# Two of four early loads asked for sooner, and batch 0's opening in a new order

## The chip, the cores and the metric

The kernel runs on one core of a Trainium2 chip. A core has five engines that run side by side, each working through its own list of instructions in order: TensorE (PE in the profile, with the loading of its weights shown as PEld), VectorE (DVE), ScalarE (ACT), GpSimd (POOL) and SyncE (SP). They meet through semaphores. Transfers between the core's memory and the chip's main memory run on 16 DMA engines; in this kernel POOL asks for the loads and SP for the copies inside the core and for the stores. The metric is the device time of one execution in microseconds (us), lower being better.

## The reference

The input x has 4 batches of 12480 rows of 128 numbers; there are 32 inducing rows I of 128 numbers and two weight matrices, w_in (128 x 2048) and w_out (2048 x 128).

```
h   = softmax(scale * I @ x^T) @ x          # per batch: 32 rows of 128
y   = softmax(scale * x @ h^T) @ h          # per batch: 12480 rows of 128
u   = y @ w_in                              # 49920 rows of 2048
out = (u * clip(u + 3, 0, 6) / 6) @ w_out   # 49920 rows of 128
```

Every row of y is a mixture of the 32 rows of h, with softmax weights. For small u the clip does nothing and the last two lines are a linear and a quadratic form of y. The kernel uses this: per batch it makes a table from h and the weights once (a linear part BD and a quadratic part Cq), and then needs for each row only products of the row's mixing weights with that table. A second path, taken only if a check of bounds at the end fails, computes everything directly; it isn't run on these inputs.

## The kernel before, in words

**Tiling.** A batch is cut into seven groups: six of 2048 rows (one load of 1 MB each) and one of 192 rows. A group of 2048 rows is four chunks of 512 rows, so that a batch has 25 chunks and the whole kernel 100.

**Three kinds of work.** *First pass* over a batch: load a group (load_x, line 207), cast it to bf16 (a_cast, line 357, written "k"), transpose it on TensorE into a bank of PSUM (a_T, line 366, "T") and copy it out (a_xT, line 375, "xT"), scores (a_scores, line 381, "s"), exponential (a_exp, line 393, "a"), and the weighted sum of rows (a_agg, line 419, "g"). After the last group this gives the denominators ("den", "n", line 403 and 451), H and its transpose HT (lines 467 to 482, with a bf16 copy HTb that ScalarE makes).
*Table* of a batch: 16 blocks, each a product dpm with a quarter of a column block of w_in (c_dpm, line 616, "dp"), its square ("q", line 631 on ScalarE, or lines 628 and 629 as a copy and a product on VectorE for the blocks named in BY_DVE), and four products with w_out (c_C, line 642, "C") into one bank cp; beside them G (line 517), hs (570, 571), L (585, 596), lt (601) and BD (606). The weights are first cast: w_in to bf16 ("wi", line 250, ScalarE), the rest that the cast leaves ("wl", line 255), w_out to bf16 ("wo", line 259).
*Second pass*: for each chunk the mixing weights TF (products bp, line 783, exponential at line 796), their products TD with d (line 807), and nine groups of products into a bank op (lines 818 and 837), which line 857 multiplies by r and line 867 stores. d is the bf16 tile dk of a group (line 762) spread over partitions by a copy inside the core that SP asks for (b_spread, line 771), six chunks ahead.

**Order.** Nothing is scheduled by a tool: each engine runs what the program text names, in that order. Batch 0's first pass and table, and the first pass of batch 1's group 0, come from the list ORDER, one token per step ("k5.1:A" is the cast of quarter 1 of group 5 on ScalarE, :D VectorE, :P GpSimd). After ORDER comes the loop over the 100 chunks ("the main loop"); it takes the second pass of chunk t and, from the list PLAN, pieces of the first pass and the table of the next batch at fixed places. In the loop SP asks at step t for the copy d of chunk t + 6.

**Banks.** TensorE writes into PSUM banks of three pools: five banks "f" (psF), two banks "o" (psO) and one for the weighted sum. In ORDER the last letter of a token on TensorE says from which pool its bank comes. A pool hands out its banks again only when the reader of the older content is done.

**Idle products.** "warmN:f" puts N products of 128x512 on a tile of zeros (line 278) into the list of TensorE, into a bank of the pool that is named; nobody reads them.

**Loads.** Five buffers of 1 MB hold loaded groups. POOL asks for batch 0's groups 1 to 4 at the start, and for groups 5 and 6 ("dx5", "dx6"), for batch 1's group 0 ("dx10"), w_in ("dwi", two halves) and w_out ("dwo", four quarters) as buffers come free. Batch 1's groups 1 to 4 are "held": the token "held" makes POOL copy one element of d of chunk 3 (the tile "seen", line 873), which waits until that copy has landed, and only then asks for the four loads. The next loads in PLAN are batch 1's group 6 in step 0 of the main loop and group 5 in step 1.

Of the kernel before, what the change touches and what calls it, by code (L numbers as in the profile page):

```python
# [28 lines left out]
LEAD = 2  # L29
AHEAD = 6  # L30
SUMG = 5
BY_DVE = (2, 6, 11)

SPLIT = (4, 5)

# [57 lines left out]
""".split()  # L93

ORDER = """
k0.0:A k0.2:D k0.1:A warm3:o T0.1:o T0.0:o xT0.1:A xT0.0:D k1.2 warm3:f s0:f a0 k1.0:D k1.1:P
T1.1:f z1:D z0:A T1.0:f z3:P xT1.1:D z2:A g0.0 xT1.0:D k2.1:P k2.2 g0.1 k2.0:D s1:f dx5 y0
T2.1:f a1 dx6 T2.0:o xT2.1:D g1.0 g1.1 k3.0:D k3.2 k3.1:D y1 dx10 T3.0:o xT2.0:A dwi warm2:f
s2:f T3.1:f dwo k4.0:D k4.1:A xT3.0:D a2 T4.0:f xT3.1:D k4.3:A g2.0 k4.2:A xT4.0:D s3:f T4.1:f
y2 a3 g2.1 xT4.1:A y3 g3.0 g3.1 s4:o k5.0:D k5.1:A k5.3:D k6:A warm2:o T5.0:o k5.2:D a4 T6:f  # L100
T5.1:f xT5.0:D xT6:A g4.0 xT5.1:D s5.0:f g4.1 y4 a5.0 bk2:P s5.1:f bk0:A s6:f g5.0 bk3:P dred
a5.1 a6 n5.0 bk1:P n5.1 wi0 g5.1 g6 n6 den bT0:o wl0:P rD H wl1:P bx0:A dall warm1:f htp:f bT1:o
HT Wd HTb bx1:D wi1 warm1:f pe1:ff HTl dH bs:f dk1 wl4:P pe0:fo W ba wo1:P dp13:o e1 dp6:f by
bg0 made wl7:P e0 q6 bg1 dk0 wo3:P dp5:f q13 sp0:f wl2:P spread0 dp15:f q5 dp2:f nf0 C6 wl3:P
C13 q15 q2 dp4:o wo0:P G0:o q4 C5 dp1:f dp0:f C15 q1 wl5:D held bp0.0:f wl6:D dp11:o q0 G1 q11
G2 TF0.0 C4 wo2:A G3 dp8:f C1 hs dp9:f q8 C0 dp14:f q9 bp0.1:f C11 C8 TF0.1 dp12:o cmax dp3:f C9
q12 half L0:f q14 L1 q3 dp10:f C2 L dp7:o TD0 q10 lt:o C3 q7 C12 BD C10 C14 C7 bp1.1:f rp0:f Cq
rp1 bp1.0:f TF1.1 TF1.0 warm2:f r0
""".split()


# [17 lines left out]
def kernel(  # L129
# [9 lines left out]
    P = nc.NUM_PARTITIONS  # L139
# [30 lines left out]
    with ExitStack() as es:  # L170
# [29 lines left out]
        def load_x(b, g):  # L200
            t0, p, n = groups[g]
            src = x[b, t0 : t0 + p * n, :].rearrange("(p i) c -> p i c", i=n)
            if n == TG:
                t = xin.tile([P, TG, C], FP32R, name="xr")
            else:
                t = xlast.tile([P, n, C], FP32R, name="xl")
            nc.gpsimd.dma_start(t[:p, :, :], src)
            xs[(b, g)] = t
# [13 lines left out]
        held = [1, 2, 3, 4]  # L222
# [86 lines left out]
        BD = []  # L309
# [49 lines left out]
        def a_T(b, g, h, how="f"):  # L359
            t0, p, n = groups[g]  # L360
            st = S[b]
            lo, hi = (0, n // 2) if h == 0 else (n // 2, n)
            xb = xbs[(b, g)]
            pt = bank(how, [P, 1024], BF16, "pt")
            for i in range(lo, hi):
                nc.tensor.transpose(pt[:, (i - lo) * p : (i - lo + 1) * p], xb[:p, i, :], ident_b[:p, :p])  # L366
            st[("pt", g, h)] = pt

        def a_xT(b, g, h, eng):
            t0, p, n = groups[g]  # L370
            lo, hi = (0, n // 2) if h == 0 else (n // 2, n)
            if ("xT", g) not in S[b]:
                S[b][("xT", g)] = (xTp if n == TG else xTl).tile([P, n * p], BF16, name="xT")
            pt = S[b].pop(("pt", g, h))
            eng(S[b][("xT", g)][:, lo * p : hi * p], pt[:, : (hi - lo) * p])  # L375

        def a_scores(b, g, how="f", lo=0, hi=TG):
            t0, p, n = groups[g]
            s1 = bank(how, [P, 512], FP32, "s1")
            for i in range(lo, min(hi, n)):  # L380
                nc.tensor.matmul(  # L381
                    s1[:p, i * M : (i + 1) * M],
                    lhsT=S[b][("xT", g)][:, i * p : (i + 1) * p],
                    rhs=I_T[:, :],
                )
            S[b][("s1", g, lo)] = s1
# [235 lines left out]
        def c_sq(jb):  # L622
            st = S[0]
            dpm = st.pop(("dpm", jb))
            sq = sqp.tile([P, 512], BF16, name="sq")
            if jb in BY_DVE:
                d32 = cst.tile([P, 512], FP32, name="d32", tag="scr")
# [251 lines left out]
        def first(kind, ix, how):  # L879
# [4 lines left out]
            i, j = (ix + [0, 0])[:2]  # L884
# [19 lines left out]
            elif kind == "T":  # L904
                a_T(0, i, j, at)
            elif kind == "xT":
                a_xT(0, i, j, eng)
            elif kind == "s":
                a_scores(0, i, at, *((8 * j, 8 * j + 8) if i == 5 else ()))
            elif kind == "a":  # L910
                a_exp(0, i, *((8 * j, 8 * j + 8) if i == 5 else ()))
            elif kind == "g":
                for h in range(2) if i == last else (j,):
                    a_agg(0, i, h)
            elif kind == "y":
                a_sum(0, i)
            elif kind == "n":
                a_den(i, *((8 * j, 8 * j + 8) if i == 5 else ()))
            elif kind == "dx":
                load_x(*((1, 0) if i == 10 else (0, i)))  # L920
            elif kind == "dwi":
                load_w_in()
            elif kind == "dwo":
                load_w_out(0, 4)
            elif kind == "held":
                gate("seen", S[0][("d", 3)][:, 0:1])
                while held:
                    load_x(1, held.pop(0))
            elif kind == "made":
                gate("made", S[0]["dH"][:, 1, 1, 0, 0:1])  # L930
            elif kind == "wi":
                w_in_cast(i)
            elif kind == "wo":
                w_out_cast(i, eng)
            elif kind == "wl":
                w_low(i, nc.vector if how == "D" else nc.gpsimd)
            elif kind == "bk":
                a_cast(1, 0, ((eng, i, i + 1),))
            elif kind == "bT":
                a_T(1, 0, i, at)  # L940
            elif kind == "bx":
                a_xT(1, 0, i, eng)
            elif kind == "bs":
                a_scores(1, 0, at)
            elif kind == "ba":
                a_exp(1, 0)
            elif kind == "bg":
                a_agg(1, 0, i)
            elif kind == "by":
                a_begin(1)  # L950
                a_sum(1, 0)
            elif kind == "dred":
                c_sum(0)
            elif kind == "HTb":
                c_HTb(0, act)
            elif kind == "htp":
                c_htp(0, at)
            elif kind in ("den", "rD", "dall", "H", "HT", "HTl", "W", "Wd"):
                {"den": c_den, "rD": c_rD, "dall": c_d, "H": c_H, "HT": c_HT, "HTl": c_HTl, "W": c_W, "Wd": c_Wd}[
                    kind  # L960
                ](0)
            elif kind == "dH":
                c_dH()
            elif kind == "pe":
                b_ep(0, i, at[0])
                b_pp(0, i, at[1])
            elif kind == "e":
                b_e(0, i)
            elif kind == "dk":
                b_dk(0, i)  # L970
                if i and "spread" in S[0]:
                    spread_rest()
            elif kind == "spread":
                for c in range(4):
                    b_spread(0, c)
                S[0]["spread"] = True
                if ("dk", 1) in S[0]:
                    spread_rest()
            elif kind == "sp":
                b_sp(0, i, at)  # L980
            elif kind == "nf":
                b_nf(0, i)
            elif kind == "rp":
                b_rp(0, i, at)
            elif kind == "r":
                b_r(0, 1)
            elif kind == "bp":
                b_bp(0, i, j, at)
            elif kind == "TF":
                b_TF(0, i, j)  # L990
            elif kind == "TD":
                b_prod(0, i)
            elif kind == "dp":
                c_dpm(i, at)
            elif kind == "q":
                c_sq(i)
            elif kind == "C":
                c_C(0, i)
            elif kind == "G":
# [331 lines left out]
```

## Time and profile before

| | us |
|---|---|
| median of 3 runs | 293.96 (293.09 to 295.51) |
| the profiled execution | 292.84 |
| its span, first to last instruction | 291.1 |
| TensorE busy in the span | 282.1 (97%) |
| VectorE busy | 231.9 (80%) |
| ScalarE busy | 227.0 (78%) |
| GpSimd busy | 130.5 (45%) |
| time around the span | 1.7 |

The page of the profile gives busy time per engine, then the chain that ended last, then the costliest groups. Two further views are used: a table of windows, which shows for each stretch of time the busy time of every engine and what the DMA engines moved, and the list of instructions in order of time, which shows when each started, how long it took, and after what idle time and whose release. Times in them count from the start of the span. A matmul's recorded duration contains its way through the array, so that several overlap; the distance from one start to the next is what it costs TensorE. The main loop starts at 42.2 us with the product of line 667 behind the last two idle products.

### The profile page before, as it was taken

How to read it: one execution, taken by the hardware profiler on the slowest of the kernel's cores; microseconds unless marked ns; L12 is line 12 of the kernel's file. 1: busy time of each engine (PE TensorE's matmuls, PEld its weight loads, DVE VectorE, ACT ScalarE, POOL GpSimd, SP SyncE). 2: the span in 40 equal slices, each digit the busy share in tenths (PEclk: the TensorE clock that was granted, in tenths of full speed). 3: DMA queues.
4: the chain of work that ended last, by engine and by line, in shares of the span. 5: the costliest groups of instructions: out<-in, count | busy, mean ns of one | idle time of the engine just before them, and what ended most of it. 6: DMA issues, size and time to landing. Idle time of an engine off the chain costs nothing.

```text
span 291.1 us, 9807 instructions
## 1 busy us (share of the span) xinstructions
PE 282.1 (97%) x3960; PEld 227.6 (78%) x3971; DVE 231.9 (80%) x495; ACT 227.0 (78%) x412; POOL 130.5 (45%) x250
## 2 busy tenths in 40 slices
PE   7999999899999999999999999999999999999993
PEld 2778667798888887978888786987887877787882
DVE  1777987789878887788898877788888887898784
ACT  2897988886889988888889887667789878777770
POOL 7465645111538899521677776100577850000000
PEclk9999999999999999999999999999999999999998
DMA  7999499698895665999838825616456566466764
GB/s 258 428 365 270 104 329 402 231 273 281 285 357 161 245 199 177 336 317 259 295 84 216 305 100 148 214 35 203 160 150 182 172 208 222 146 216 217 229 227 156
DMA packets 25137, 66.69 MB, mean 229 GB/s; under 512 B 3168, under 2 KB 18304, under 8 KB 19072
## 3 DMA queue, kind: packets, MB, share of 16 engines
q1 hardware_dynamic: 18880, 39.40, 41.9%
q0 software_dynamic: 6160, 26.61, 28.5%
q8 instruction: 32, 0.52, 0.7%
q14 instruction: 17, 0.14, 0.2%
q10 hardware_dynamic: 48, 0.02, 0.0%
HBM read 27.67 MB, written 25.56 MB: 183 GB/s over the span
## 4 chain that ended last, share of the span: by engine, by line
PE 80%; DMA 11%; DVE 5%; issue 1%; ACT 1%; ACTq 0%; DVEq 0%; POOLq 0%
PE op L837 29%; PE bp L783 13%; PE op L818 8%; PE hnd L419 7%; PE pt L366 5%; DMA xr<-in_x_dram 5%; PE cp L642 5%; DMA out_dram<-os 4%; PE s L381 2%; DMA d<-dk 2%; PE sp L687 2%; PE pp L748 2%; PE ep L667 2%; PE lp L585 1%; PE gp L517 1%
## 5 line engine op out<-in xcount | busy, mean ns | idle before, releaser
L796 ACT ACTIVATE TF<-bp 128x512 bf16<-128x512 f32 (+1 forms) x200 | 115.6, 589 | 32.8 <-PE bp L783 18.9
L837 PE MATMUL op<-Cq,TF 128*128 128x128 bf16 (+1 forms) x784 | 100.3, 221 | 0.1
L837 PE MATMUL op<-Cq,TD 128*128 128x128 bf16 (+1 forms) x784 | 98.6, 219 | 0.0
L857 DVE TENSOR_TENSOR os<-op,r_all 128x512 f32<-128x512 f32 x96 | 65.9, 687 | 20.5 <-PE op L837 18.3
L807 DVE TENSOR_TENSOR TD<-TF,d 128x1024 bf16<-128x1024 bf16 (+1 forms) x100 | 74.8, 748 | 0.2
L837 PEld LDWEIGHTS <-TF 128*128 128x128 bf16 (+1 forms) x784 | 56.1, 98 | 21.2 <-issue 11.0
L783 PE MATMUL bp<-xT,W 128*128 128x512 bf16 (+1 forms) x193 | 72.3, 375 | 0.1
L837 PEld LDWEIGHTS <-TD 128*128 128x128 bf16 (+1 forms) x784 | 60.4, 98 | 0.0
L818 PE MATMUL op<-BD,nf 128*128 128x512 f32 (+1 forms) x100 | 54.7, 547 | 0.0
L357 POOL CAST xb<-xr 128x512 bf16<-128x512 f32 x33 | 25.1, 778 | 29.7 <-DMA xr<-in_x_dram 17.5
L544 POOL COPY gate<-TD 128x1 bf16<-128x1 bf16 x48 | 14.1, 294 | 51.2 <-DVE TD L807 49.2
L547 POOL TENSOR_TENSOR dg<-G 128x256 f32<-128x256 f32 x48 | 35.6, 741 | 0.0
L546 POOL TENSOR_TENSOR dg<-G 128x256 f32<-128x256 f32 x48 | 31.5, 656 | 6.9 <-DVE r_all L736 3.6
L554 ACT ACTIVATE sq<-dg 128x512 bf16<-128x512 f32 x48 | 30.0, 629 | 3.8 <-POOL dg L547 2.1
L419 PE MATMUL hnd<-xr,a 128*32 128x128 f32 x384 | 30.6, 227 | 0.0
L366 PE MATMUL pt<-ident_b,xb 128*128 128x128 bf16 x392 | 29.6, 219 | 1.0 <-DVE xb L357 0.5
L419 PEld LDWEIGHTS hnd<-xr,a 128*32 128x32 f32 x384 | 24.8, 109 | 2.7 <-issue 1.3
L366 PEld LDWEIGHTS <-xb 128*128 128x128 bf16 x392 | 23.2, 98 | 4.6 <-issue 1.6
L726 PE MATMUL rp<-one,nf 128*128 128x4 f32 (+1 forms) x100 | 25.6, 257 | 0.9 <-ACT dk L762 0.9
L375 ACT COPY xT<-pt 128x1024 bf16<-128x1024 bf16 (+1 forms) x24 | 22.4, 950 | 2.8 <-PE pt L366 2.6
L642 PE MATMUL cp<-w_out_b,sq 128*128 128x128 bf16 x256 | 22.4, 220 | 0.1
L726 PEld LDWEIGHTS rp<-one,nf 128*128 128x128 f32 (+1 forms) x100 | 18.9, 189 | 3.7 <-ACT dk L762 1.3
(131 smaller groups left out, 417.2 us busy)
## 6 DMA issues: line engine op xcount, KB each, us to landing
xr<-in_x_dram POOLq DMA_DIRECT2D x23, 1024.0 KB, 8.1
out_dram<-os SPq DMA_DIRECT2D x23, 1024.0 KB, 4.6
d<-dk SPq DMA_DIRECT2D x96, 128.0 KB, 4.4
os<-in_x_dram SPq DMA_DIRECT2D x1, 1024.0 KB, 5.7
w_in_r<-in_moe_w_in_dram POOLq DMA_DIRECT2D x2, 512.0 KB, 9.9
w_out_r<-in_moe_w_out_dram POOLq DMA_DIRECT2D x4, 256.0 KB, 10.8
out_dram<-os SPq DMA_DIRECT2D x4, 256.0 KB, 3.4
xl<-in_x_dram POOLq DMA_DIRECT2D x4, 96.0 KB, 7.0
```

The source lines that it names most:

```text
L366: nc.tensor.transpose(pt[:, (i - lo) * p : (i - lo + 1) * p], xb[:p, i, :], ident_b[:p, :p])
L419: nc.tensor.matmul(st["hnd"][:M, :C], lhsT=st[("a1", g)][:p, i * M : (i + 1) * M], rhs=xs[(b, g)][:p, i, :], start=(g == 0 and i == 0), st ...
L546: nc.gpsimd.tensor_sub(dg[:, 0], stepped(G2, jb, 0, 1, 0), stepped(G2, jb, 2, 0, 2))
L547: nc.gpsimd.tensor_sub(dg[:, 1], stepped(G2, jb, 1, -1, 0), stepped(G2, jb, 10, 0, 2))
L642: nc.tensor.matmul(st["cp"][:, k * C : (k + 1) * C], lhsT=sq[:, k * P : (k + 1) * P], rhs=w_out_b[:, jc, :], start=(k0 == 0 and k == 0), s ...
L726: nc.tensor.matmul(st["rp"][:p, at : at + S_], lhsT=nf[:R, j * p : (j + 1) * p], rhs=one4[:R, :S_], skip_group_check=True,)
L783: nc.tensor.matmul(st[("bp", c, k)][:, :w], lhsT=st["W"][:, k].rearrange("p m i -> p (m i)"), rhs=st[("xT", g)][:, j * w : (j + 1) * w],)
L796: nc.scalar.activation(st[("x", c)][:, k, :w], bp[:, :w], ACT.Exp, scale=scale)
L807: nc.vector.tensor_mul(u[:, :, :w], t[:, :, :w], d[:, :w].unsqueeze(1).to_broadcast([P, 2, w]))
L818: nc.tensor.matmul(op[:p, : S_ * C], lhsT=st[("nf", g)][:R, j * p : (j + 1) * p], rhs=st["BD"][:R, : S_ * C], start=True, stop=False, skip ...
L837: nc.tensor.matmul(op[:p, s * C : (s + 1) * C], lhsT=T[k][:, s * p : (s + 1) * p], rhs=st["Cq"][:, k, :], start=False, stop=(s == S_ - 1 a ...
L857: nc.vector.tensor_mul(ot[:p, j * S_ : (j + 1) * S_, :], op[:p, : S_ * C].rearrange("p (s c) -> p s c", c=C), r_all[:p, b, c, :S_].unsquee ...
```

## The change

The list ORDER is replaced by another with the same steps, but for three things.

- **Loads.** Two new tokens, dx11 and dx12, ask for batch 1's groups 1 and 2 ahead of the gate: dx11 stands behind dwo, dx12 some steps further. The token "held" still waits for d of chunk 3, and then asks for the two that are left, groups 3 and 4.
- **Idle products.** The list had warm3:o, warm3:f, warm2:f, warm2:o, warm1:f, warm1:f and warm2:f (14 products); it now has warm4:f, warm3:f and warm1:f (8 products), all in the pool of five.
- **The rest of the order.** The sequence of the table's blocks is another one, the squares on VectorE are those of blocks 6, 9 and 14 instead of 2, 6 and 11, and some casts and copies change their engine (all four casts of w_out are on GpSimd, one of them was on ScalarE; both casts of w_in stand ahead of HTb on ScalarE, the second stood behind it; half_rows, four small steps of VectorE, moves from behind hs to ahead of H).

PLAN and the main loop are unchanged.

```
-BY_DVE = (2, 6, 11)
+BY_DVE = (6, 9, 14)
 ...
-k0.0:A k0.2:D k0.1:A warm3:o T0.1:o T0.0:o xT0.1:A xT0.0:D k1.2 warm3:f s0:f a0 k1.0:D k1.1:P
 ...
-T2.1:f a1 dx6 T2.0:o xT2.1:D g1.0 g1.1 k3.0:D k3.2 k3.1:D y1 dx10 T3.0:o xT2.0:A dwi warm2:f
-s2:f T3.1:f dwo k4.0:D k4.1:A xT3.0:D a2 T4.0:f xT3.1:D k4.3:A g2.0 k4.2:A xT4.0:D s3:f T4.1:f
-y2 a3 g2.1 xT4.1:A y3 g3.0 g3.1 s4:o k5.0:D k5.1:A k5.3:D k6:A warm2:o T5.0:o k5.2:D a4 T6:f
-T5.1:f xT5.0:D xT6:A g4.0 xT5.1:D s5.0:f g4.1 y4 a5.0 bk2:P s5.1:f bk0:A s6:f g5.0 bk3:P dred
-a5.1 a6 n5.0 bk1:P n5.1 wi0 g5.1 g6 n6 den bT0:o wl0:P rD H wl1:P bx0:A dall warm1:f htp:f bT1:o
-HT Wd HTb bx1:D wi1 warm1:f pe1:ff HTl dH bs:f dk1 wl4:P pe0:fo W ba wo1:P dp13:o e1 dp6:f by
-bg0 made wl7:P e0 q6 bg1 dk0 wo3:P dp5:f q13 sp0:f wl2:P spread0 dp15:f q5 dp2:f nf0 C6 wl3:P
 ...
-rp1 bp1.0:f TF1.1 TF1.0 warm2:f r0
+k0.1:A k0.2:D k0.0:D warm4:f T0.1:o T0.0:o xT0.1:A xT0.0:D k1.2 warm3:f s0:f k1.0:D k1.1:P z0:D
 ...
+a1 dx6 T2.1:o xT2.0:A g1.0 k3.0:D g1.1 k3.2 xT2.1:D dx10 y1 warm1:f s2:o dwi T3.1:f k3.1:D a2
+T3.0:f xT3.1:A k4.1:D dwo g2.0 k4.0:D g2.1 xT3.0:D k4.3:A k4.2:D s3:f y2 T4.0:f a3 T4.1:f
+xT4.0:A g3.0 y3 g3.1 xT4.1:D s4:o k5.0:D k5.1:A k5.2:D dx11 k5.3:A T5.0:o k6:D a4 T5.1:f xT5.0:D
+T6:f g4.0 xT5.1:A xT6:D y4 s5.0:f g4.1 bk2:P a5.0 dred s5.1:f s6:f g5.0 bk3:P a5.1 a6 n5.0 dx12
+bk1:A n5.1 half wi0 bk0:P n6 den g5.1 rD dall g6 wi1 bT1:o wl0:P H htp:o bT0:f HTb HT bx1:A Wd
+bx0:D pe1:ff HTl dH bs:f dk1 pe0:fo ba wl1:D wo3:P dp6:f dp12:o dk0 by wl3:P bg0 e0 q6:D spread0
+bg1 wl6:P e1 dp7:f sp0:f wo1:P q7:A dp13:o dp14:f nf0 wl7:P q12:A dp1:f C6 q14:D C7 made q13:A
 ...
+bp1.1:f bp1.0:f Cq TF1.1 rp0:f rp1 TF1.0 r0
 ...
             elif kind == "dx":
-                load_x(*((1, 0) if i == 10 else (0, i)))
+                load_x(i // 10, i % 10)
+                if i > 10:
+                    held.remove(i % 10)
```

More of the change, by code (lines that the diff above doesn't have):

```diff
@@ L95 @@
 ORDER = """
-k0.0:A k0.2:D k0.1:A warm3:o T0.1:o T0.0:o xT0.1:A xT0.0:D k1.2 warm3:f s0:f a0 k1.0:D k1.1:P
-T1.1:f z1:D z0:A T1.0:f z3:P xT1.1:D z2:A g0.0 xT1.0:D k2.1:P k2.2 g0.1 k2.0:D s1:f dx5 y0
-T2.1:f a1 dx6 T2.0:o xT2.1:D g1.0 g1.1 k3.0:D k3.2 k3.1:D y1 dx10 T3.0:o xT2.0:A dwi warm2:f
-s2:f T3.1:f dwo k4.0:D k4.1:A xT3.0:D a2 T4.0:f xT3.1:D k4.3:A g2.0 k4.2:A xT4.0:D s3:f T4.1:f
-y2 a3 g2.1 xT4.1:A y3 g3.0 g3.1 s4:o k5.0:D k5.1:A k5.3:D k6:A warm2:o T5.0:o k5.2:D a4 T6:f
-T5.1:f xT5.0:D xT6:A g4.0 xT5.1:D s5.0:f g4.1 y4 a5.0 bk2:P s5.1:f bk0:A s6:f g5.0 bk3:P dred
-a5.1 a6 n5.0 bk1:P n5.1 wi0 g5.1 g6 n6 den bT0:o wl0:P rD H wl1:P bx0:A dall warm1:f htp:f bT1:o
-HT Wd HTb bx1:D wi1 warm1:f pe1:ff HTl dH bs:f dk1 wl4:P pe0:fo W ba wo1:P dp13:o e1 dp6:f by
-bg0 made wl7:P e0 q6 bg1 dk0 wo3:P dp5:f q13 sp0:f wl2:P spread0 dp15:f q5 dp2:f nf0 C6 wl3:P
-C13 q15 q2 dp4:o wo0:P G0:o q4 C5 dp1:f dp0:f C15 q1 wl5:D held bp0.0:f wl6:D dp11:o q0 G1 q11
-G2 TF0.0 C4 wo2:A G3 dp8:f C1 hs dp9:f q8 C0 dp14:f q9 bp0.1:f C11 C8 TF0.1 dp12:o cmax dp3:f C9
-q12 half L0:f q14 L1 q3 dp10:f C2 L dp7:o TD0 q10 lt:o C3 q7 C12 BD C10 C14 C7 bp1.1:f rp0:f Cq
-rp1 bp1.0:f TF1.1 TF1.0 warm2:f r0
+k0.1:A k0.2:D k0.0:D warm4:f T0.1:o T0.0:o xT0.1:A xT0.0:D k1.2 warm3:f s0:f k1.0:D k1.1:P z0:D
+a0 T1.1:f z2:D z3:P z1:A T1.0:f xT1.1:A g0.0 xT1.0:D k2.1:P g0.1 k2.2 k2.0:D s1:f dx5 y0 T2.0:f
+a1 dx6 T2.1:o xT2.0:A g1.0 k3.0:D g1.1 k3.2 xT2.1:D dx10 y1 warm1:f s2:o dwi T3.1:f k3.1:D a2
[5 more added lines that the diff above has]
+bg1 wl6:P e1 dp7:f sp0:f wo1:P q7:A dp13:o dp14:f nf0 wl7:P q12:A dp1:f C6 q14:D C7 made q13:A
+wl2:P dp3:f G0:f q1:A C12 wo0:P C13 q3:A dp15:o W wo2:P dp10:o C14 q15:A wl4:D dp8:f wl5:P C1
+q10:A dp9:f bp0.0:f held G1 q9:D TF0.0 dp0:o G2 q8:A G3 C3 C10 hs dp2:o q0:A dp4:f C9 bp0.1:f
+q4:A C8 C0 q2:A cmax dp5:f L0:o TF0.1 L1 q5:A dp11:f C4 L C2 TD0 q11:A lt:o C15 C5 BD C11
+bp1.1:f bp1.0:f Cq TF1.1 rp0:f rp1 TF1.0 r0
 """.split()
```

## The prediction, made before the changed kernel was run

> **What bounds the kernel now.** First the page: busy time and the chain that ended last.
>
> ```profile
> PE 282.1 (97%) x3960; PEld 227.6 (78%) x3971; DVE 231.9 (80%) x495; ACT 227.0 (78%) x412; POOL 130.5 (45%) x250
> PE 80%; DMA 11%; DVE 5%; issue 1%; ACT 1%; ACTq 0%; DVEq 0%; POOLq 0%
> ```
>
> TensorE is busy for 282.1 of 291.1 us. Behind the opening it has no slack, so whatever moves the start of the main loop, or stops TensorE after it, moves the end by as much. The table of windows says where it stops, and what the DMA engines do there:
>
> ```profile
> 26.00:28.00 2.00, 1.98 (x25) 1.24 (x27) 1.40 (x6) 1.38 (x3) 1.30 (x2) 1.00 2.13 254
> 28.00:30.00 2.00, 2.00 (x37) 0.99 (x31) 2.00 (x6) 2.00 (x4) 1.25 (x2) 1.00 0.28 41
> 30.00:32.00 2.00, 1.85 (x21) 1.10 (x19) 1.97 (x4) 2.00 (x6) 2.00 (x5) 1.00 0.00 0
> ...
> 40.00:42.00 2.00, 2.00 (x26) 1.61 (x26) 1.42 (x3) 0.79 (x3) 0.58 (x2) 1.00 1.04 410
> ...
> 50.00:52.00 2.00, 1.15 (x11) 0.65 (x10) 1.30 (x3) 0.64 (x2) 0.00 (x0) 1.00 1.05 380
> ```
>
> (Columns: window, length, busy time of PE, PEld, DVE, ACT, POOL, granted clock, DMA share, GB/s.) From 28 to 32 us the DMA engines move almost nothing; from 40 on they run at some 400 GB/s, still at 380 in the last window, and there TensorE loses 2.00 - 1.15 = 0.85 us. The chain, in order of time, names the cause:
>
> ```profile
> 42.88 0.61 DVE TD L807
> ...
> 43.50 6.29 DMA d<-dk
> 49.79 1.49 issue
> ...
> 51.37 0.61 ACT dk L762
> ...
> 52.02 0.27 PE rp L726
> ```
>
> The copy d of chunk 7, asked for at 43.50, takes 6.29 us. Until it has landed, line 762 can't overwrite the dk tile that it reads; ScalarE stands still, a bank stays occupied, and the next product on TensorE (rp) starts at 52.02. The view of waits has ScalarE's part:
>
> ```profile
> ACT dk L762 <- PE bp L783: 1.6, 1, 1.6
> ```
>
> So line 762 was due at 51.37 - 1.6 = 49.8. The traffic is that of the four held loads and the two after them; in the list of POOL's instructions:
>
> ```profile
> 20.55 0.81 POOL L246 DMA_DIRECT2D w_out_r<-in_moe_w_out_dram  x1 [1.75 <-DMA xr<-in_x_dram]
> 29.52 0.81 POOL L259 CAST w_out_b<-w_out_r 128x512 bf16<-128x512 f32 x1
> 31.80 1.30 POOL L255 TENSOR_TENSOR w_in_l<-w_in_r,w_in_b 128x256 bf16<-128x256 f32 x2
> 35.93 0.19 POOL L873 COPY seen<-d 128x1 bf16<-128x1 bf16 x1 [2.28 <-DMA d<-dk]
> 36.17 2.20 POOL L207 DMA_DIRECT2D xr<-in_x_dram  x4
> 41.42 1.18 POOL L357 CAST xb<-xr 128x512 bf16<-128x512 f32 x2 [3.04 <-DMA xr<-in_x_dram]
> 44.05 1.18 POOL L357 CAST xb<-xr 128x512 bf16<-128x512 f32 x2 [1.45 <-DMA xr<-in_x_dram]
> 45.69 0.54 POOL L207 DMA_DIRECT2D xr<-in_x_dram  x1
> ```
>
> The loads land one per 44.05 - 41.42 = 2.63 us, the first 5.25 us after it was asked for.
>
> **Part 1, the loads.** dx11 stands behind the last quarter of w_out, asked for at 20.55 + 0.81 = 21.4; the buffer that it fills and the load whose semaphore it takes over (batch 0's group 6) are free by then. dx12 follows behind two casts of batch 1's group 0, near 25. Both queue behind w_out, whose landing the first window puts near 28 to 29.7, so that they fall into the idle stretch and end near 32 and 34.6 (2.63 each). They share that time with the copies d of chunks 0 to 5. Before, d of chunk 3 was seen at 35.93; I take 36.5 now, with 35.5 and 38.5 as bounds (no contention, or one load more ahead of it). The gate then asks for two loads, which land near 41.8 and 44.4. POOL no longer waits for groups 1 and 2, so the loads of groups 6 and 5 are asked for near 40 instead of up to 45.69: the stream ends near 47 instead of 52. Two loads left out of it are 2 x 2.63 = 5.3 us, which agrees. For d of chunk 7 I have rows for a full stream (6.29) and for all copies:
>
> ```profile
> d<-dk SPq DMA_DIRECT2D x96, 128.0 KB, 4.4
> ```
>
> With half of its time in the stream it lands by 43.9 + 4.4 to 5.3 = 48.3 to 49.2 and, with the 1.49 us of issue behind it, lets line 762 go at 49.8 to 50.7, where it is due at 49.8. Of 1.6 us that ScalarE stood still, 0 to 0.9 stays; TensorE stood still for only 0.85 of them, having work in hand for the rest, so its stall is gone or, at the late end, 0.9 - (1.6 - 0.85) = 0.15. I take **-0.85 us** (bounds: 0, if the copy is no sooner, and -0.85; nothing else of the main loop stops TensorE that early).
>
> *A rule against this.* The Trainium skill, DMA: Bandwidth & Descriptors, section "Queues, rings and completion order", says that a DMA engine takes its queues in turn, packet by packet. By it the copies of chunks 0 to 3 would pay for groups 1 and 2 running beside them; with equal shares that is an estimate of their own 0.5 MB once more, some 1.3 us. No row here has copies beside two loads only; the 6.29 against the 4.4 agrees in kind. It would put the gate at 37.2, inside my bounds, and is part of the third rival.
>
> **Part 2, the order, from the last load to the main loop.** Here two things are gained and lost again.
>
> ```profile
> 15.47 1.07 POOL L240 DMA_DIRECT2D w_in_r<-in_moe_w_in_dram  x2
> ...
> 20.34 0.62 ACT L357 CAST xb<-xr 128x512 bf16<-128x512 f32 x1
> 21.17 0.59 ACT L393 ACTIVATE a<-s 128x512 fp32r<-128x512 f32 x1
> 21.62 1.14 PE L366 MATMUL pt<-ident_b,xb 128*128 128x128 bf16 x18
> 27.53 0.19 ACT L482 CAST HTb<-htp 128x32 bf16<-128x32 f32 x1
> 27.61 1.06 ACT L250 CAST w_in_b<-w_in_r 128x1024 bf16<-128x1024 f32 x1
> ```
>
> *Gained:* group 5's transposes start at 21.62, though their casts end at 20.34 + 0.62 = 20.96. warm2:o had one bank of the pool of two and s4 the other, which is free only near the end of its exponential (21.17 + 0.59). Without these idle products they start at 21.0. From there to the denominators TensorE's own work decides, so H could be 0.6 us sooner, less 0.1 to 0.2 for the cast k5.3 that ScalarE now makes behind k5.1.
>
> *Lost:* HTb needs H, but on ScalarE it now stands behind both casts of w_in. The second half was asked for at 15.47 + 1.07 / 2 = 16.0 and lands as the view of that tile says:
>
> ```profile
> DMA to landing us min/median/max: 9.4/9.9/10.4
> ```
>
> The later of the two halves is taken to be the maximum: 16.0 + 10.4 = 26.4, and the cast takes 1.06: HTb starts at 27.5, where it started before (27.53). Then bx1 runs behind HTb, which holds up the scores bs; against this stands that the 1.06 of the second cast is out of the way there.
>
> From the first product C on, TensorE's work is the sum. Costs per step, from the chain:
>
> ```profile
> 31.98 0.62 PE cp L642 x8
> ...
> 33.11 0.23 PE cp L642 x4
> 33.35 0.43 PE dpm L616 x2
> 34.43 0.60 PE gp L517 x24
> 37.98 0.95 PE lp L585 x16
> 39.60 0.41 PE lt L601 x2
> ```
>
> Before, C begins at 31.98 with 5 of 16 dp done: 16 C x 0.23 = 3.7, 11 dp x 0.215 = 2.4, G 1.2, L 0.95, lt 0.41, four bp at 0.22 and two rp 1.3, two idle products 0.43; in all 10.4, to 42.4. The main loop's first product:
>
> ```profile
> 42.18 0.40 PE L667 MATMUL ep<-xT,HTb 128*32 128x512 bf16 x4
> ```
>
> The sum meets it within 0.2, so TensorE has no stall in it worth a number. In the new list 6 dp are done ahead of C and the idle products at the end are gone: 3.7 + 2.15 + 1.2 + 0.95 + 0.41 + 1.3 = 9.7. C can begin when w_out's second quarter is cast. How long w_out's quarters take to land, in the view of that tile:
>
> ```profile
> DMA to landing us min/median/max: 9.1/10.8/10.9
> ```
>
> POOL, in order, first casts the last quarter, which lands at 20.55 + 9.1 = 29.65 (the minimum taken for the last, which has the least ahead of it), then makes two rests wl, then casts the second: 29.65 + 0.81 + 1.30 + about 0.6 (an estimate: less than the 0.81, as the pairs of casts at 41.42 and 44.05 took 1.18) = 32.4.
>
> 32.4 + 9.7 = 42.1, and about 0.1 of waits for squares on VectorE: **42.2, as before**. VectorE loses half_rows from its full stretch but has its third square ahead of hs; the two about cancel, and L hides behind the four C and dp that stand between lp and lt. ScalarE loses one cast of w_out and isn't late. Bounds for this part: -0.6 (what the transposes gain comes through) to +0.6 (lt and C each late by their margin).
>
> **Part 3, idle products.** Six fewer, 6 x 0.215 = 1.3 us of TensorE; four stood where it waited anyway, the last two (0.43) are in the sum above. The long wait that is new is from bT0 to HTb, 26.7 to 27.7, about 1 us.
>
> **Sum.** 292.84 (profiled: span 291.1 and 1.74 around it) - 0.85 + 0 = 292.0. The median of the runs shown is 1.1 above the profiled execution, all three of them above it; on their scale the sum is 293.96 - 0.85 = **293.1**, and I give the time on that scale.
>
> **The rivals**, on the same scale.
>
> 1. *The opening gets shorter too.* If w_in's second half lands sooner, or the list hides its cast, the 0.6 of the transposes and the 0.43 of the idle products come through: 293.1 - 0.6 to - 1.0 = 292.1 to 292.5. For it: VectorE and ScalarE each lose a step there. Against: HTb's time above.
> 2. *No gain.* The stream merely moves forward: the loads of groups 5 and 6 take the place of the two that left, d of chunk 7 still meets them and the stall stays, or another copy (chunk 6) meets it instead: 294.0.
> 3. *Slower: w_out's last quarter lands late.* POOL's list now hangs on it, with seven casts behind it and C behind the second of w_out. If the early loads or the copies share the DMA engines with it (a share of 2.13 at only 254 GB/s from 26 to 28 says that w_out is slow to move as it is), each us that it lands after 29.65 is a us for C and the main loop. Bound: one load's time, 2.63. With 1.2 to 2.6: 293.1 + 1.2 to 2.6 = 294.3 to 295.7.
> 4. *The clock falls.* The first eleven idle products took 4.35 us, 0.40 each, where the dp of the same shape cost 0.215 later; in the last window, with TensorE idle for 4.66 us of 11.10, the clock is 0.87:
>
> ```profile
> 1.20 4.35 PE L278 MATMUL wp<-wake 128*128 128x512 bf16 x11 [1.20 <-DVE wake L266]
> ```
>
> ```profile
> 14.00:16.00 2.00, 1.44 (x20) 1.04 (x18) 1.36 (x3) 1.95 (x2) 1.05 (x3) 1.00 1.04 344
> ...
> 280.00:291.10 11.10, 6.44 (x83) 5.32 (x81) 6.34 (x20) 2.69 (x6) 0.00 (x0) 0.87 0.54 204
> ```
>
> So TensorE is slow when it has idled. Halving its speed over a stretch like the first (4.35) costs up to 2.2 us: 293.1 + 2.2 = 295.3. Against it: the new wait is near 1 us, and from 14 to 16 TensorE was idle for 0.56 of 2 at a clock of 1.00. The Trainium skill, TensorE: Matmul & The Clock Gate, "The HAM clock gate", has the clock fall after an idle window of about 3.4 us; by that it stays, and no row of this case shows where the limit is.
>
> **How the numbers follow.** Forecast 0.50 (293.1, alone 292.6 to 293.8), rival 1 0.19, rival 2 0.15, rival 3 0.12, rival 4 0.04. The range takes in the first three and the near half of the fourth, with 0.5 for the runs' own spread below: 291.4 to 295.0; 0.1 is left out. One per cent (2.9 us) is about what a measurement of this kernel can tell from no change: faster by it would need the stall, the transposes and all idle products at once (0.05); slower, rivals 3 and 4 at their far ends (0.06); within it 0.89.
>
> **What would show it.** Right: DMA engines busy from 28 to 35, quiet by 48; d of chunk 7 under 5.5 us; no 0.85 us hole of TensorE near 51; HTb at 27.5; the first product of the main loop at 42.2. Wrong: that product elsewhere by over 0.6 us, w_out's casts on POOL behind 30.5, a clock under 1.00 between 20 and 45, or a new wait of the main loop on d of chunks 4 to 6.

## The result, and the profile after

The kernel after takes 291.76 us (median of 20 runs, 290.91 to 293.67) against 293.36 for the kernel before beside it (20 runs, 292.4 to 295.73): a ratio of 0.9944, 95% interval 0.9921 to 0.9966, a gain of 1.0 to 2.3 us where 0.85 was forecast. Two later comparisons of the same two kernels gave 0.9972 (0.9945 to 0.9998) and 0.9992 (0.9969 to 1.0014). The mean of the three is 0.9969, some 0.9 us: about what was forecast, and less than the first comparison alone says. The ratios leave out runs that are over 1.5% above the fastest of their kernel (one of 35 of the kernel before in two comparisons, two of 12 of one_load); the medians have all runs.

The page of the profile after (span; busy time; granted clock in 40 slices; the chain that ended last by engine):

```profile
span 291.5 us, 9804 instructions
...
PE 282.5 (97%) x3965; PEld 227.9 (78%) x3965; DVE 231.2 (79%) x498; ACT 226.9 (78%) x408; POOL 129.0 (44%) x251
...
PEclk9999799999999999999999999999999999999997
...
PE 90%; DMA 7%; ACT 1%; POOL 0%; DVE 0%; issue 0%; POOLq 0%
```

DMA has fallen from 11% of the chain to 7%, and a slice near 30 us has a clock of 0.7, which before had not. The table of windows of the same execution has both:

```profile
26.00:28.00 2.00, 1.02 (x14) 0.66 (x11) 0.17 (x1) 1.58 (x2) 0.67 (x1) 1.00 2.44 308
28.00:30.00 2.00, 1.27 (x18) 0.48 (x18) 1.34 (x5) 1.71 (x4) 0.00 (x0) 0.74 1.44 401
30.00:32.00 2.00, 2.00 (x24) 0.68 (x20) 1.61 (x5) 1.62 (x4) 1.09 (x2) 0.50 1.10 413
32.00:34.00 2.00, 2.00 (x21) 1.50 (x20) 1.44 (x3) 1.35 (x3) 2.00 (x4) 0.91 0.87 289
...
48.00:50.00 2.00, 2.00 (x31) 1.69 (x28) 1.79 (x5) 1.79 (x4) 0.53 (x1) 1.00 0.41 138
50.00:52.00 2.00, 2.00 (x27) 1.29 (x26) 1.71 (x3) 2.00 (x5) 0.09 (x1) 1.00 0.33 66
```

From 28 to 34 us, where the DMA engines had all but rested until 32, they now move 290 to 410 GB/s; from 48 on they are nearly quiet, and TensorE has no hole near 51 any more. But from 26 to 30 it is busy for only 2.29 of 4 us, and behind that its clock falls: the columns 0.74, 0.50 and 0.91 lack (0.26 + 0.50 + 0.09) x 2 us = 1.7 us of clock. The list of instructions says what it stood still for:

```profile
27.46 1.04 ACT L250 CAST w_in_b<-w_in_r 128x1024 bf16<-128x1024 f32 x1 [0.26 <-DMA w_in_r<-in_moe_w_in_dram]
28.42 0.18 ACT L482 CAST HTb<-htp 128x32 bf16<-128x32 f32 x1
28.65 0.40 PE L667 MATMUL ep<-xT,HTb 128*32 128x512 bf16 x4 [1.63 <-ACT HTb L482]
...
30.91 0.61 POOL L259 CAST w_out_b<-w_out_r 128x512 bf16<-128x512 f32 x1 [2.94 <-DMA w_out_r<-in_moe_w_out_dram]
...
37.76 0.19 POOL L873 COPY seen<-d 128x1 bf16<-128x1 bf16 x1 [0.94 <-DMA d<-dk]
...
43.80 0.40 PE L667 MATMUL ep<-xT,HTb 128*32 128x512 bf16 x4
...
51.69 0.61 ACT L762 ACTIVATE dk<-pp 128x512 bf16<-128x512 f32 x1
```

HTb stands behind the second cast of w_in, whose load landed 1.0 us later than forecast, and TensorE waits 1.63 us for it. The main loop starts at 43.80 instead of 42.18. From there to the end of the span, one row for before and one for after:

```profile
42.18:291.10 248.92, 243.21 (x3408) 199.16 (x3412) 202.43 (x434) 195.87 (x359) 105.13 (x189) 0.99 0.68 219
```

```profile
43.80:291.50 247.70, 243.27 (x3413) 199.00 (x3412) 202.19 (x436) 196.20 (x360) 100.62 (x183) 0.99 0.66 212
```

TensorE does the same work (243.2 us) in 1.22 us less. So this execution lost 1.62 in the opening and won 1.22 behind it: 0.4 slower in span than the profiled one of before, though the medians say faster. It took 293.30 us, among the slowest of its 20. The 18 others with a mean granted clock of 0.994 or more have a median of 291.64; if their loop is as long, their main loop starts near 43.80 - (293.30 - 291.64) = 42.1 (an estimate; all three profiles of this kernel are of executions with a lower clock). What has to be found out: whether the loads alone give the 1.2, what the new order is worth, and when the clock falls.

### The profile page after: what moved, and what is told of

Same layout as the page of the kernel before. It is cut to its first block, busy times and chain, and to the rows that moved or that the text cites. A ratio compares the mean times of both kernels' runs of the same rounds, so it can differ in the third digit from the quotient of the medians.

```text
span 291.5 us, 9804 instructions
## 1 busy us (share of the span) xinstructions
PE 282.5 (97%) x3965; PEld 227.9 (78%) x3965; DVE 231.2 (79%) x498; ACT 226.9 (78%) x408; POOL 129.0 (44%) x251
## 4 chain that ended last, share of the span: by engine, by line
PE 90%; DMA 7%; ACT 1%; POOL 0%; DVE 0%; issue 0%; POOLq 0%
PE op L837 32%; PE bp L783 15%; PE op L818 9%; PE hnd L419 7%; PE pt L366 6%; PE cp L642 5%; DMA w_in_r<-in_moe_w_in_dram 4%; PE s L381 3%; DMA xr<-in_x_dram 3%; PE sp L687 3%; PE pp L748 3%; PE ep L667 2%; PE gp L517 2%; PE dpm L616 1%; PE lp L585 1%; PE rp L726 1%
## 5 line engine op out<-in xcount | busy, mean ns | idle before, releaser
L783 PE MATMUL bp<-xT,W 128*128 128x512 bf16 (+1 forms) x200 | 74.8, 375 | 0.0
L357 POOL CAST xb<-xr 128x512 bf16<-128x512 f32 x33 | 24.4, 758 | 30.5 <-DMA xr<-in_x_dram 14.2
L547 POOL TENSOR_TENSOR dg<-G 128x256 f32<-128x256 f32 x48 | 34.9, 726 | 0.0
L546 POOL TENSOR_TENSOR dg<-G 128x256 f32<-128x256 f32 x48 | 30.7, 639 | 6.5 <-DVE r_all L736 3.6
L375 ACT COPY xT<-pt 128x1024 bf16<-128x1024 bf16 x25 | 25.1, 1015 | 3.2 <-PE pt L366 3.0
L697 DVE CUSTOM_DVE_ANT_0 nf<-e,sp 128x512 fp32r<-128x512 f32 (+1 forms) x28 | 17.2, 613 | 5.6 <-PE sp L687 5.6
```

What stands on the lines that cost most here:

```text
L546: nc.gpsimd.tensor_sub(dg[:, 0], stepped(G2, jb, 0, 1, 0), stepped(G2, jb, 2, 0, 2))
L547: nc.gpsimd.tensor_sub(dg[:, 1], stepped(G2, jb, 1, -1, 0), stepped(G2, jb, 10, 0, 2))
L783: nc.tensor.matmul(st[("bp", c, k)][:, :w], lhsT=st["W"][:, k].rearrange("p m i -> p (m i)"), rhs=st[("xT", g)][:, j * w : (j + 1) * w],)
```

## The experiments

Three comparisons of four kernels each, on three chips; "before" below is the kernel before, run among them (35 runs each: 293.04, 292.81 and 292.11 us). Two numbers are read from each profile, which is that of one execution: the start of the main loop's first product, and the time from it to the end of the span (the loop). The clock of the last column is the mean granted clock of TensorE in a run. Of each edit only the tokens beside it are shown.

| kernel | median, us | ratio to before (95%) | first product | loop | runs at a clock of 0.993 or less |
|---|---|---|---|---|---|
| before | see above | 1 | 42.18 | 248.92 | 18 of 105 |
| after (three times) | 291.76, 292.59, 292.02 | 0.9944, 0.9972, 0.9992 | 43.80, 43.86, 43.48 | 247.70, 247.84, 247.82 | 10 of 44 |
| loads_only | 292.26 | 0.9955 (0.9927 to 0.9983) | 42.52 | 247.48 | 0 of 12 |
| order_only | 292.75 | 0.9960 (0.9927 to 0.9993) | 43.28 | 249.32 | 3 of 12 |
| htb_first | 292.10 | 0.9965 (0.9940 to 0.9990) | 42.64 | 247.76 | 3 of 12 |
| xt3_first | 291.83 | 0.9950 (0.9917 to 0.9983) | 41.90 | 247.90 | 1 of 12 |
| xt3_htb (twice) | 291.28, 291.65 | 0.9934 (0.9903 to 0.9965), 0.9976 (0.9949 to 1.0004) | 41.71, 41.71 | 247.79, 247.89 | 2 of 24 |
| hole_filled | 291.95 | 0.9967 (0.9937 to 0.9996) | 42.40 | 247.90 | 0 of 12 |
| warm_f | 292.72 | 1.0010 (0.9970 to 1.0049) | 42.11 | 248.59 | 2 of 12 |
| one_load | 292.73 | 1.0001 (0.9971 to 1.0031) | 41.68 | 247.52 | 3 of 12 |
| dk_four | 291.16 | 0.9978 (0.9950 to 1.0005) | 41.54 | 247.46 | 1 of 12 |

### The loads without the order, the order without the loads

loads_only is the kernel before with the two loads ahead of the gate (and the three lines that serve dx11 and dx12):

```
-k5.3:D k6:A
+k5.3:D dx11 k6:A
 ...
-n5.0 bk1:P
+n5.0 dx12 bk1:P
```

> The kernel before with one part of the change: dx11 and dx12 put into its old list (dx11 between k5.3 and k6, dx12 behind n5.0), the gate left with two loads; order, engines, idle products and BY_DVE as before. Theory A (as forecast: the stall of 0.85 us near 51 goes, the opening is no shorter): 0.85 us under the kernel before (ratio 0.997), d of chunk 7 under 5.5 us, no idle TensorE from 50 to 52. Theory B (the loads bring everything that was measured, 1.6 us): ratio 0.9945. Theory C (the early loads delay w_out or the copies d of chunks 0 to 5 in the opening and give the gain back): ratio 1.000 or above, the main loop's first product later than 42.2.

order_only is the kernel after without them; the gate then asks for all four:

```
-k5.2:D dx11 k5.3:A
+k5.2:D k5.3:A
 ...
-n5.0 dx12
+n5.0
```

> The changed kernel without dx11 and dx12: all four loads behind the gate again, the new list otherwise kept. Theory A (the order is worth nothing): ratio 1.000 to the kernel before, the 0.85 us stall near 51 still there. Theory B' (the order and the fewer idle products shorten the opening): 0.6 to 0.8 us under the kernel before, ratio 0.9975, with HTb and the main loop's first product earlier by as much, where the profile is of an execution without a slow clock. Theory D (HTb behind both casts of w_in costs time): TensorE waits 1 us or more ahead of the product ep of group 1, w_in's second half decides, and the ratio is over 1.000.

The two rows of the loop, loads_only first:

```profile
42.52:290.00 247.48, 242.75 (x3408) 199.05 (x3412) 201.80 (x434) 195.73 (x359) 100.78 (x184) 1.00 0.66 213
```

```profile
43.28:292.60 249.32, 243.67 (x3408) 198.94 (x3412) 203.52 (x436) 196.53 (x360) 106.01 (x190) 0.99 0.68 219
```

With the loads the loop is 247.5, without them 249.3, and ScalarE's wait is back in order_only:

```profile
ACT dk L762 <- PE bp L783: 1.6, 1, 1.6
```

So the shorter loop is the loads' work, and they do it in the old order as well. One expectation failed: in loads_only the copy d of chunk 7 took 6.6 us, not under 5.5, and ScalarE still stood idle for 0.29 us ahead of line 762, but TensorE had no hole. In the medians both kernels are 0.4% ahead of before, with intervals that overlap each other and that of the kernel after beside them (0.9972), so that the two gains can't be added; the profiles don't show where order_only would gain, since its opening is 1.1 us longer in the execution that was profiled, the longest of its twelve. Its gain stays unexplained.

### HTb ahead of the second cast of w_in; the kernel after again

htb_first is the kernel after with one token moved:

```
-g6 wi1 bT1:o
+g6 bT1:o
 ...
-HTb HT bx1:A Wd
+HTb HT wi1 bx1:A Wd
```

> The changed kernel with one token moved: the second cast of w_in stands behind HTb on ScalarE, as it did before. Theory D (HTb held up by w_in's landing costs the opening): HTb starts at 26.4 to 27.3 instead of 28.4, TensorE's wait ahead of ep of group 1 falls from 1.6 us to under 0.9, no slow clock between 28 and 34, the main loop starts 0.5 to 1.2 us sooner than in the changed kernel, ratio to the kernel before 0.990 to 0.993. Rival (the second cast only moves its 1.04 us elsewhere on ScalarE: bx1, dk and the scores come later by it): no difference to the changed kernel, ratio 0.9945.

> The changed kernel again, for the comparison with the others on the same chip and for a second profile. If the slow clock of the first profile (0.50 from 30 to 32) belongs to some executions only, this one may show 1.00 there and a main loop that starts 1.0 to 1.7 us sooner than 43.8; if it belongs to the kernel, it shows again. Ratio 0.9945 either way.

The wait for HTb is gone in htb_first (its first use is at 27.64). The median is 0.5 us under that of the kernel after beside it, but the ratios (0.9965 and 0.9972) can't be told apart, and the 0.990 to 0.993 that was expected isn't reached. Both profiles have another wait, not seen at this size in the first profile of after (0.49 there): TensorE's scores of group 3 wait for a copy xT on VectorE, which stands behind two casts of chunk group 4 that wait for that group's load. In after_again, and then in htb_first, from the list of TensorE's instructions:

```profile
16.17 1.15 PE L419 MATMUL hnd<-xr,a 128*32 128x128 f32 x16
19.36 0.60 PE L381 MATMUL s<-I_T,xT 128*128 128x32 bf16 x16 [2.04 <-DVE xT L375]
19.80 1.87 PE L366 MATMUL pt<-ident_b,xb 128*128 128x128 bf16 x16
```

```profile
15.96 1.16 PE L419 MATMUL hnd<-xr,a 128*32 128x128 f32 x16
19.01 0.56 PE L381 MATMUL s<-I_T,xT 128*128 128x32 bf16 x16 [1.90 <-DVE xT L375]
19.43 1.05 PE L366 MATMUL pt<-ident_b,xb 128*128 128x128 bf16 x16
```

Here is the clock: the sixteen transposes take 1.87 us behind the one wait and 1.05 behind the other, which is nearly as long. From 20 to 22 us the two windows say 0.50 and 1.00:

```profile
20.00:22.00 2.00, 2.00 (x22) 2.00 (x20) 1.23 (x3) 1.74 (x3) 0.81 (x2) 0.50 1.11 373
```

```profile
20.00:22.00 2.00, 2.00 (x43) 1.89 (x41) 1.76 (x4) 2.00 (x4) 1.48 (x2) 1.00 1.05 375
```

The load of group 4 isn't asked for any later in these kernels. VectorE's cast of it starts at 16.5 to 16.8 in the first profile of after, in loads_only and in before, and at 17.6 to 17.9 in htb_first, order_only and after_again (15.65 in the third profile of after): the landing varies between executions of the same kernel, and the list has TensorE wait for it.

### Group 3's copy ahead of that load; both edits together

xt3_first is the kernel after with xT3.0 moved ahead of the two casts; xt3_htb has htb_first's edit too:

```
-T3.0:f xT3.1:A k4.1:D dwo g2.0 k4.0:D g2.1 xT3.0:D k4.3:A
+T3.0:f xT3.1:A xT3.0:D k4.1:D dwo g2.0 k4.0:D g2.1 k4.3:A
```

> The kernel after with VectorE's copy xT of group 3 ahead of the two casts of chunk 4 (it stood behind them, and they wait for chunk 4's load). Theory A (the new order is worth less than it could be because group 3's scores wait for chunk 4's load through that copy, 1.9 to 2.0 us in three of four profiles, and the clock falls in a part of the executions after that wait): the wait of s behind xT near 17 to 19 us under 0.7 us, the denominators (dps, L451) by 25.7 us, main loop's first product 42.0 to 43.2, at most one run in ten under a clock of 0.993, median 0.4 to 0.9 us under the kernel after, ratio to before 0.992 to 0.9945. Theory B (the copy only passes the wait on: the transposes of group 4 wait for the same load): the wait moves to pt, L366, with the same 1.5 to 2 us, median as the kernel after, ratio 0.995 to 0.997, a fifth of the runs under 0.993.

> The same, and also the cast of the second half of w_in behind HTb and HT on ScalarE. Theory A: no wait for HTb and none over 0.7 us for xT; main loop's first product 40.7 to 42.0, ratio to before 0.989 to 0.993, and no run under a clock of 0.993. Theory B (the opening is bound by the loads whatever the order: H by chunk 5 and the leftover, the first C by w_out): first product 42.2 or later, ratio 0.994 to 0.997.

In the profile of xt3_first group 4 landed late again (its cast at 17.88), and what is left of the wait stands before group 4's own transposes:

```profile
18.89 1.15 PE L366 MATMUL pt<-ident_b,xb 128*128 128x128 bf16 x16 [0.97 <-DVE xb L357]
```

0.97 instead of 1.9 to 2.0: theory A, with half of theory B's wait left over. Both first products (41.90, 41.71) are earlier than in any profile of after; in neither did the clock fall there. The ratio of xt3_first (0.9950) is within the noise of after's, that of xt3_htb (0.9934) the best of all; so it was run once more beside after:

> The kernel after with both edits of the opening once more (group 3's copy ahead of chunk 4's casts, second cast of w_in behind HTb and HT), beside the kernel after on the same chip. Theory A (the two waits were what the opening lost): ratio 0.991 to 0.995, 0.4 to 1.0 us under the kernel after, no run at a clock under 0.993. Theory B (0.9934 was chance): within 0.3 us of the kernel after.

> The kernel after, unchanged, a third time: ratio 0.994 to 0.998; a tenth to a third of its runs at a clock of 0.989 to 0.991 and 293.2 or more, the others 290.9 to 292.9; first product of the main loop 41.8 to 44.2.

0.9976 against 0.9992: 0.37 us ahead, with overlapping intervals, and two of its runs had the low clock. So theory A failed in the ratio and in the clock, and that xt3_htb beats the kernel after isn't shown. The second profile also says what is left to gain there: group 4 landed early in it and HTb was ready at 25.86 instead of 26.75, yet the first product is at 41.71 again. The first product C starts at 32.22, after 0.48 us of waiting for the cast of w_out on GpSimd (32.21 in the other profile). From there the landing of w_out decides, as the prediction's sum had it (32.4) and as theory B has it.

### Idle products where TensorE waits

```
-k4.2:D s3:f y2
+k4.2:D warm8:f s3:f y2
```

> The kernel after with eight idle products (8 x 0.22 = 1.8 us) on TensorE between group 2's hnd products and group 3's scores, that is where three of four profiles have the wait of 1.9 to 2.0 us. Theory A (the clock falls because TensorE stood still there): every run at a clock of 0.994 or more and no run over 293.2; where chunk 4 lands early the products cost up to 1.3 us, so the median is 291.8 to 292.8, ratio 0.995 to 0.999. Theory B (the clock falls by the chip's own lights, whatever TensorE does there): a fifth of the runs under 0.993 again, at 293.5 and more, median 292.5 to 293.3.

```profile
17.25 1.90 PE L278 MATMUL wp<-wake 128*128 128x512 bf16 x8
18.98 0.56 PE L381 MATMUL s<-I_T,xT 128*128 128x32 bf16 x16
```

In this profile group 4 landed early (cast at 16.46), so there was no long wait to fill; what counts is the runs. No run of 12 had a clock under 0.996 and none was over 293.07, as theory A has it. Chance alone would do that too in (34/44)^12, about 5% of cases, if these runs were like after's 44.

### The idle products' bank alone

```
-k6:A warm2:o T5.0:o
+k6:A warm2:f T5.0:o
```

> The kernel before with one edit: the two idle products ahead of group 5's transposes take their bank from the other pool. Theory A (this alone changes nothing at the end, because HTb waits for w_in): group 5's transposes 0.4 to 0.6 us earlier (21.0 to 21.2), main loop's first product 41.9 to 42.3, the wait at L726 for dk still 0.8 to 0.9, ratio 0.998 to 1.001. Rival (what the order gained, about 0.4 us, is this part): first product 41.5 to 41.8, ratio 0.996 to 0.998.

No gain at the end (1.001): first product at 42.11, ScalarE's wait near 51 as before. The transposes of group 5 start only at 21.55 (21.62 before), since the two idle products are still ahead of them; in the first profile of after, which hasn't got them, they start at 21.05. What was expected there comes with taking the products away, not with their bank.

### What in the loads made the stall

one_load moves only dx11. dk_four moves no load, and gives line 762 a fourth buffer, so that it doesn't wait for the copy d of chunk 7 (the room comes from the tile of zeros, whose 128 columns are read four times):

```
-        dpk = es.enter_context(tc.tile_pool(name="dpk", bufs=3))
+        dpk = es.enter_context(tc.tile_pool(name="dpk", bufs=4))
```

> The kernel before with one of the two loads moved (dx11 between the casts of chunk 5's group; the gate asks for three). If the copy of chunk 7 is late because the stream of loads runs beside it, half the dose gives part of the gain: the stream ends near 50 instead of 52.5, line 762 waits 0.3 to 1.2 us instead of 1.6, the hole of TensorE before L726 is 0 to 0.5 instead of 0.86, and from the main loop's first product to the end of the span 247.8 to 248.5 (248.6 to 249.3 without early loads, 247.5 to 247.9 with two); ratio 0.9965 to 0.999. Rival (the gain comes from the batch-1 groups being there sooner for VectorE and POOL, not from the copy): hole still 0.8 to 0.9 and length 248.5 or more.

> The kernel before, no load moved, with a fourth buffer for dk (line 762 then has no copy d to wait for; the idle products read a tile of 128 columns four times over, which makes the room). If the copy alone makes the stall: no wait at L762 and no hole of TensorE near 51, length from the main loop's first product to the end 247.6 to 248.2, first product 41.9 to 42.5, ratio 0.996 to 0.9985, the same as two early loads gave (0.9955). Rival (a late copy holds up something else next, the products of chunk 7 themselves or the next group's dk): the hole comes back within 5 us at 0.5 or more, length 248.5 or more, ratio 0.9985 to 1.001.

The copy d of chunk 7 by the view of that tile, from the asking to the moment that its waiters see (the 6.29 of the chain and most of the 1.49 of issue behind it), in before, after, loads_only, one_load and dk_four:

```profile
L771 SPq DMA_DIRECT2D d<-dk x1: 543/543/543, 43.5 to 43.5; - x1
...
DMA to landing us min/median/max: 7.7/7.7/7.7
```

```profile
L771 SPq DMA_DIRECT2D d<-dk x1: 542/542/542, 45.4 to 45.4; - x1
...
DMA to landing us min/median/max: 4.8/4.8/4.8
```

```profile
L771 SPq DMA_DIRECT2D d<-dk x1: 543/543/543, 43.7 to 43.7; - x1
...
DMA to landing us min/median/max: 6.6/6.6/6.6
```

```profile
L771 SPq DMA_DIRECT2D d<-dk x1: 543/543/543, 43.0 to 43.0; - x1
...
DMA to landing us min/median/max: 4.5/4.5/4.5
```

```profile
L771 SPq DMA_DIRECT2D d<-dk x1: 543/543/543, 42.7 to 42.7; - x1
...
DMA to landing us min/median/max: 7.7/7.7/7.7
```

dk_four is the one that decides: the copy is as late as before, 7.7 us, and yet the loop is 247.46 and TensorE waits for nothing from 44 to 60 us. So it is the wait for a free dk buffer that cost the time, not the late d itself, and the two early loads gain nothing in the loop that one buffer doesn't gain as well. (The interval of its ratio, 0.9950 to 1.0005, just takes in 1.) The hole's price is read from starts, before first and dk_four second:

```profile
50.56 0.59 PE L818 MATMUL op<-BD,nf 128*128 128x512 f32 x1
52.02 0.27 PE L726 MATMUL rp<-one,nf 128*128 128x4 f32 x1 [0.86 <-ACT dk L762]
```

```profile
49.94 0.58 PE L818 MATMUL op<-BD,nf 128*128 128x512 f32 x1
...
50.36 0.17 PE L726 MATMUL rp<-one,nf 128*128 128x4 f32 x1
```

From the one start to the other it is 1.46 us with the stall and 0.42 without: 1.04, where the idle time says 0.86.

In the profile of one_load one early load does it too (4.5 us; loop 247.52), where a part of the stall was expected to be left. What sets the copy's time stays open: with early loads it took 3.7 to 6.6 us in the ten profiles, without them 7.3 to 7.8 in four, but more loads moved didn't mean a faster copy (4.5 with one, 6.6 with two in the same order). In its times one_load shows no gain, not even among its nine runs at a clock above 0.993 (292.03 against 292.07 for the kernel before). The profiled execution, 291.00, is one of its fastest; the runs spread from 290.95 to 297.87, and what makes the slower ones slow no profile shows.

## Why the prediction was right, and where not

- **The stall (-0.85 forecast): right in its mechanism, mis-sized.** The hole is gone, and dk_four and order_only show from both sides that the copy of chunk 7 made it, through line 762. The loop is shorter by 1.1 to 1.2 us (248.92 against 247.70 to 247.84) instead of 0.85. The term that was too small is the hole itself: I took 2.00 - 1.15 from the busy time, which counts recorded durations that reach past the next start; from start to start it is 1.04, and the stretch to the second rp is another 0.10 longer in before (1.06 against 0.96 in dk_four). The copy, with the issue behind it, got faster than my range in after (4.8 where 7.7 was, so 2.9 us off, while I had it 1.0 to 1.9 off) and not in loads_only (6.6, so 1.1 off); the stall was gone either way, since TensorE had work in hand, as forecast.
- **The opening (0 forecast): near for most executions only, and this by an estimate.** For those with the full clock the times give a first product near 42.1, against 42.2 forecast. In all three profiles of after it is at 43.5 to 43.9, but all three are of executions in which the clock fell, as it did in 10 of 44. What failed is the step that took one landing time for each load: "16.0 + 10.4 = 26.4" for w_in's second half was 27.4 in the first profile, HTb 28.42 instead of 27.5, the last quarter of w_out was cast at 30.91 instead of 29.65 (rival 3's sign), and group 4's load, which the sum left out, landed between 15.65 and 17.94 in the three profiles of after (the start of VectorE's cast).
- **The clock (rival 4, 0.04).** Here the forecast was wrong. I had "the new wait is near 1 us" and the clock staying; in the third profile of after the wait was 0.97 and the clock fell:

```profile
27.96 0.40 PE L667 MATMUL ep<-xT,HTb 128*32 128x512 bf16 x4 [0.97 <-ACT HTb L482]
...
29.04 0.60 PE L381 MATMUL s<-I_T,xT 128*128 128x32 bf16 x16 [0.20 <-DVE xT L375]
29.57 0.62 PE L667 MATMUL ep<-xT,HTb 128*32 128x512 bf16 x4
```

  (0.40 for the four products at 27.96, 0.62 for four like them at 29.57.) A clock of 0.993 or less stands in 10 of 44 runs of after, which are some 1.6 us longer (median 293.4 against 291.8 for the others). The price that I gave it, up to 2.2 us, was near, though I took it from the first idle products (0.40 us each), where the granted clock reads 1.00. The kernel before has such a clock in 18 of 105 runs, which are longer by 2.4 to 3.1 us in the three comparisons, so the change in the median is small; no profile of before caught one, and where its clock falls stays open.
- **The gate (36.5, bounds 35.5 to 38.5).** "seen" was at 37.76 in after, inside; less the 1.6 by which that opening was late, near 36. In loads_only, with the old opening, it was 36.93. Loads beside the copies did cost the gate 1.0 us against the 35.93 of before: the first two copies d took 4.4 and 4.0 us there, 2.7 and 2.8 in before.
- **Rival 1 (the opening gets shorter too)** came out only with xt3_first and xt3_htb: 41.7 to 41.9 against the 42.18 of before. That isn't proof of a better order: the old one, in one_load and dk_four, had its first product at 41.68 and 41.54, so the profiles of one order differ by as much. These two stem from the third comparison, in which the kernel before was 0.7 to 0.9 us faster than in the other two; the smallest gain (0.9992) stems from it too.
- **The sum.** 293.1 on the scale of the runs then shown, 291.76 measured. Of these 1.3 us, 0.6 is the scale (a median of 293.96 in three runs of the kernel before, 293.36 in 20) and 0.75 the larger gain; the time lies under the band that I gave the forecast alone (292.6 to 293.8). The first comparison gives -1.6, the three together about -0.9. That the mean agrees with -0.85 is partly luck: the loop of the profiles gained 1.1 to 1.2, and what became of the rest isn't shown. The -1.6 is partly the luck of the kernel before, seven of whose 20 runs were over 295 (9, 6 and none of 35 later). Among the runs at a clock above 0.993 the kernel after is 0.77 and 0.45 us ahead in the two later comparisons.

## What to carry to other kernels

A transfer as late as before cost nothing once its source had one buffer more (dk_four): look for the buffer that a late reader keeps occupied, and try one more before moving the transfers. Read the price of a hole from starts, not from idle time. In an opening that is fed by loads, the landing times vary by 1 to 2 us between executions; put nothing that is ready behind a cast that waits for a load, and treat the first product of the main loop as a range. One profile shows one execution: read its time against the spread of the runs before reading its stages.

## What the runs showed of the hardware that was not expected

**The clock fell to one half after TensorE had stood still for 1 to 2 us, and for the same time in all four profiles.** The windows of after_again, order_only and after_third in which it was under 1.00, in this order (that of after is above):

```profile
18.00:20.00 2.00, 0.64 (x19) 0.64 (x20) 2.00 (x5) 0.57 (x2) 0.95 (x2) 0.86 1.14 362
20.00:22.00 2.00, 2.00 (x22) 2.00 (x20) 1.23 (x3) 1.74 (x3) 0.81 (x2) 0.50 1.11 373
22.00:24.00 2.00, 2.00 (x40) 2.00 (x39) 1.26 (x4) 1.27 (x3) 0.47 (x1) 0.79 1.26 377
```

```profile
18.00:20.00 2.00, 0.84 (x24) 0.84 (x25) 2.00 (x5) 0.54 (x2) 0.82 (x1) 0.99 1.06 338
20.00:22.00 2.00, 2.00 (x23) 2.00 (x21) 1.58 (x4) 2.00 (x4) 0.74 (x1) 0.50 1.09 394
22.00:24.00 2.00, 2.00 (x38) 1.96 (x37) 0.84 (x4) 0.94 (x2) 0.00 (x0) 0.65 1.12 397
```

```profile
28.00:30.00 2.00, 1.71 (x32) 0.80 (x32) 1.97 (x7) 1.68 (x3) 0.00 (x0) 0.78 1.22 395
30.00:32.00 2.00, 2.00 (x16) 0.93 (x9) 1.62 (x4) 1.67 (x4) 1.77 (x3) 0.50 1.08 414
32.00:34.00 2.00, 2.00 (x19) 1.39 (x17) 1.10 (x2) 0.97 (x3) 2.00 (x5) 0.87 0.86 241
```

What lacks to 1.00, times 2 us, is 1.70, 1.72 and 1.70, and 1.70 in after: each time 3.4 us at half speed. The standstills before were 2.04, 1.90, 0.97 and 1.63 us; behind the 0.97 two shorter stops, 0.29 us together, came before the fall. That of htb_first, 1.90, brought no fall. So the length of the wait doesn't decide it alone. That the standstill is the cause is argued from this order in time; the runs of hole_filled speak for it, but two runs of xt3_htb, whose edits shorten both waits, had the low clock too.

The Trainium skill, TensorE: Matmul & The Clock Gate, "The HAM clock gate", says that activity is watched in windows of 3.4 us that run freely, and that half speed comes after an idle window. The 3.4 us at half speed agree with one such window, and windows that run freely would explain why the same wait does it in one execution and not in the other (no run here shows their edges). That a whole window must be idle doesn't agree: 0.97 us of standstill, 1.26 with the two stops behind it, was enough once, and the measurement decides.
